# Attention and two MoE layers on one core: weight conversions moved out of three steps, four weight pieces moved behind the first MoE's last chunks

## The chip, the cores and the metric

One core of a Trainium2 chip runs the whole program. The metric is the device time of one execution in microseconds, as the median of several. The profiler took one execution of its own; its trace is read below, with times in us from the span's start.

## What is computed

The reference in short (4 batches, 8 heads, 576 positions, head width 64; then 2304 tokens of 512):

```python
scores = q @ k.T / sqrt(64) + decay(cumsum(log f))    # causal
x = softmax(scores) @ v                               # heads joined: 2304 x 512
h = maximum(maximum(x @ w1, x @ w2), x @ w3)          # 512 -> 768
x = h @ w_out                                         # 768 -> 512
h = x @ w_in                                          # 512 -> 2048
g = (a0 + a1*h + a2*h**2 + a3*h**3) / (1 + |b0|*|h| + |b1|*h**2 + 1e-6)
out = g @ w_out2                                      # 2048 -> 512
```

The weights arrive as 64-bit floats, so the kernel converts them itself, with integer operations on the bits. For accuracy most products are done in three matmuls, with a high and a low half of each operand.

## The kernel before

**Attention.** A *pair* is two heads of one batch and one or both groups of query positions (group 0: 320 columns, group 1: 256). Batch 0 comes first, as eight pairs of one group each: pairs 0 to 3 do group 0, pairs 4 to 7 group 1; batches 1 to 3 have four pairs of both groups each. Every head and group of a pair is a *slot*: slots 0 and 1 are pair 0, slots 6 and 7 are pair 3, the fourth. The main loop goes over steps. In step s the scores of slot s are computed (L388 to L391 on TensorE, row maximum on VectorE at L392, exponential on ScalarE at L399), slot s-1 is transposed (L432, evacuated at L434), and slot s-2 is multiplied with `v` when it is the second head of its pair (L448). So pairs 0 to 3 have their attention in steps 3, 5, 7 and 9. ScalarE then copies the high half of `x` (L455) and VectorE subtracts the low half (L456). For pairs 0 to 3 each bank is preceded by two matmuls that only keep TensorE exercised (L84).

**First MoE.** When all four pairs of a batch and group have their `x`, 22 units are put in a queue: 18 `h` units (six chunks `fc` of 128 columns times three weights, 12 matmuls each, L482 to L484) and four output units (L508 to L510). A running maximum goes through ScalarE (L488) and VectorE (L490); the third weight of a chunk leaves `hh`, the high half by ScalarE (L494) and the low half by GpSimd, or, in the tail, by VectorE (L496). `fill` is called six times in a step and places units at a steady pace: for the first group of batch 0 they go from step 9 to step 24.

**Conversions.** `conv` lists 30 of them: 18 of `w1` (the three input weights, 512 KB each) and 12 of `wo` (the output weight, 256 KB each). One conversion is an `Abs` on ScalarE (L181), four bit operations on VectorE (L186, L187, L188, L191), a copy for the high half on ScalarE (L197) and a subtraction for the low half on GpSimd (L200). `h` unit i needs item i; the output units need all of `wo`. `fill` also runs the conversions: `conv_due` adds 0.15 at each call in steps 0 to 6 and 0.5 from step 7 on. Two items are done before the loop. The raw data is loaded on SyncE's queue (L167) two items ahead; a raw `w1` piece takes one of six buffers of the tag `x2`, a raw `wo` piece one of eight of `x1`. From step 32 on, `conv2` does the second MoE's output weight by the same stages.

**Tail.** After the steps 44 units of the first MoE are left, group 0 and 1 of the last batch. Twelve are placed at once. Then a loop goes over 32 conversions of the second MoE's `w_in` (`conv3`, two pieces for each of the 16 chunks of 128 columns, four loads ahead) and places one unit behind every second of them; then come the units that remain. The second MoE follows: for each tile of tokens and each of 16 chunks `product` (L738 to L740), a gate on ScalarE and VectorE (L747 to L771) and `moe2_o` (L787 to L789) three chunks later.

**Who sets the order.** The program text gives each instruction a priority, and a planner, which simulates the engines with times of its own, lays down each engine's stream: of what is ready, the earlier in the text first, and the evacuations of the first MoE ahead of their place. On the chip each engine works off its stream in order. `keep_in_program_order` pins some instructions (the raw loads among them) to the order of the text. `tc.issue_after(ins)` puts an edge from `ins` to each instruction in its block that runs on the same engine: these come later in that engine's stream. It adds no semaphore.

Of the kernel before, what the change touches and what calls it, by code (L numbers as in the profile page):

```python
# [8 lines left out]
F32 = mybir.dt.float32  # L9
F32R = mybir.dt.float32r  # L10
I32 = mybir.dt.int32
AF = mybir.ActivationFunctionType
ALU = mybir.AluOpType
# [24 lines left out]
def kernel(  # L38
    ctx: ExitStack, tc: tile.TileContext, q, k, v, f, w1, w2, w3, w_out, m2_in, m2_out, m2_a, m2_b, out
):  # L40
    nc = tc.nc
    B, H, S, D = q.shape
# [5 lines left out]
    NF1 = FF1 // P  # L48
    NF2 = FF2 // P
    NPAIR = H // 2  # L50
    NB = len(Q0)

    def r32(ap):
        return ap.bitcast(F32)
# [67 lines left out]
    LOOK, WHOLE, PRE = 2, 6, 2  # L122
# [36 lines left out]
    E_LO, E_HI = 2.0**-15, float.fromhex("0x1.dffffep+16")  # L159

    raws = {}

    def load_raw(src, nm_):
        shape = list(src.shape)
# [4 lines left out]
    def stages(split, src, nm_, pool, tag, bufs, pin):  # L169
        shape = list(src.shape)  # L170
        at = {}

        def held(ins):
            return tc.keep_in_program_order(ins) if pin else ins

        def magnitude():
            raw = raws.pop(nm_)
            raw = raw.rearrange("p c (f t) -> p c f t", t=2)
            at["low"], at["top"] = raw[:, :, :, 0], raw[:, :, :, 1]
            at["t"] = pool.tile(shape, I32, name=f"cv_{nm_}", tag=tag, bufs=bufs)  # L180
            held(nc.scalar.activation(at["t"].bitcast(F32), at["top"].bitcast(F32), AF.Abs))  # L181

        def bits():
            t, low, top = at["t"], at["low"], at["top"]
            tf = t.bitcast(F32)
            held(nc.vector.tensor_scalar(tf, tf, E_LO, E_HI, op0=ALU.max, op1=ALU.min))  # L186
            nc.vector.tensor_scalar(t, t, 0x07FFFFFF, 3, op0=ALU.bitwise_and, op1=ALU.logical_shift_left)  # L187
            nc.vector.scalar_tensor_tensor(  # L188
                out=t, in0=low, scalar=29, in1=t, op0=ALU.logical_shift_right, op1=ALU.bitwise_or
            )  # L190
            nc.vector.scalar_tensor_tensor(  # L191
                out=t, in0=top, scalar=-0x40000000, in1=t, op0=ALU.bitwise_and, op1=ALU.bitwise_or
            )

        def high():
            at["hi"], at["lo"] = split()
            held(nc.scalar.activation(at["hi"], at["t"].bitcast(F32), AF.Copy))  # L197

        def low():
            held(nc.gpsimd.tensor_tensor(at["lo"], at["t"].bitcast(F32), r32(at["hi"]), op=ALU.subtract))  # L200

        return [magnitude, bits, high, low]
# [46 lines left out]
    def pipelined(work, look, begun=False):  # L249

        n = len(work)

        def go(i):
            for j in range(0 if i == 0 and not begun else i + look + (i == 0), min(i + look + 1, n)):
                work[j][0]()
            work[i][1]()

        return [lambda i=i: go(i) for i in range(n)]
# [99 lines left out]
    class Unit:  # L358
# [77 lines left out]
        def attend(self):  # L436

            p, h, g = self.pair, self.h, self.g
            if h == 0:
                return  # L440
            lo, hi = GQ[g]
            w = hi - lo
            ot = exercised(ps_o.tile([P, 512], F32, name=f"o_{self.nm}", tag="o"), p.n)
            order = list(GCH[g].items())
            with tc.high_priority():
                for j, (c, (col, q0)) in enumerate(order):
                    for i in (1, 0):
                        mm = nc.tensor.matmul(  # L448
                            ot[SIDES[i][0], q0 - lo : w], p.v[:, c, i], p.pt[g][:, i, col : col + hi - q0],
                            start=(j == 0), stop=(j == len(order) - 1),  # L450
                        )
                        if (j, i) != (0, 1):
                            pinned(mm)
            x = mpool.tile([P, 2, w], F32R, name=f"x_{self.nm}", tag=f"x{g}", bufs=(6, 8)[g])
            out_ = nc.scalar.activation(x[:, 0], ot[:, :w], AF.Copy)  # L455
            nc.vector.tensor_tensor(x[:, 1], ot[:, :w], r32(x[:, 0]), op=ALU.subtract)  # L456
            xt[p.b, p.hp, g] = x
            if p.b == 0:
                last["x"] = out_.ins


    hs = {}
# [12 lines left out]
    def moe1_h(b, g, fc, j):  # L475
        w = GQ[g][1] - GQ[g][0]
        nm_ = f"{b}_{g}_{fc}"
        xs = [xt[b, dc, g] for dc in range(NDC)]
        wh, wl = w1t[fc]
        hp_ = hbank(f"h{j}_{nm_}")  # L480
        for dc in reversed(range(NDC)):
            nc.tensor.matmul(hp_[:, :w], wh[:, j, dc], xs[dc][:, 1], start=(dc == NDC - 1), stop=False)  # L482
            nc.tensor.matmul(hp_[:, :w], wh[:, j, dc], xs[dc][:, 0], start=False, stop=False)  # L483
            nc.tensor.matmul(hp_[:, :w], wl[:, j, dc], xs[dc][:, 0], start=False, stop=(dc == 0))  # L484
        with tc.high_priority():
            nxt = mpool.tile([P, 320], F32, name=f"m{j}_{nm_}", tag="mx", bufs=3)
            if j == 0:
                nc.scalar.activation(nxt[:, :w], hp_[:, :w], AF.Copy)  # L488
            else:
                nc.vector.tensor_tensor(nxt[:, :w], cur[0][:, :w], hp_[:, :w], op=ALU.max)  # L490
            cur[0] = nxt
            if j == 2:
                hh = mpool.tile([P, 2, 320], F32R, name=f"hh_{nm_}", tag="hh", bufs=6)
                nc.scalar.activation(hh[:, 0, :w], nxt[:, :w], AF.Copy)  # L494
                eng = nc.gpsimd if tail["n"] is None else nc.vector
                eng.tensor_tensor(hh[:, 1, :w], nxt[:, :w], r32(hh[:, 0, :w]), op=ALU.subtract)  # L496
                hs[b, g, fc] = hh

    def moe1_o(b, g, dc):
# [17 lines left out]
    def moe1_units(b, g):  # L517
# [10 lines left out]
    conv = [  # L528
        (lambda fc=fc, j=j: load_raw(*raw_w1(fc, j)), lambda fc=fc, j=j: convert_w1(fc, j))
        for fc in range(NF1)  # L530
        for j in range(3)
    ]
# [2 lines left out]
        for fc in range(NF1)  # L535
        for z in range(2)
    ]
    ahead = [load_ for load_, _ in conv[: LOOK + 1]]
    conv = pipelined(conv, LOOK, True)
    wps = [(c, z) for c in range(NF2) for z in range(2)]  # L540
    conv2 = []
    for i, cz in enumerate(wps):
# [9 lines left out]
    units = []  # L552
    ready, ends = {}, {}
    NFILL = 6
    for n, p in enumerate(pairs):
        if p.hp == NPAIR - 1:
            at = first.get(n + 1, len(slots)) + 1
# [4 lines left out]
    state = {"m": 0, "of": 1, "n": 0}  # L562
# [22 lines left out]
    state["c"] = state["c2"] = 0.0  # L585

    def conv_due(step):
        state["c"] += 0.15 if step < 7 else 0.5
        return NCONV - int(state["c"])

    pairs[0].load()
# [14 lines left out]
    for step in range(len(slots) + 2):  # L606
        u = slots[step] if step < len(slots) else None
        t = slots[step - 1] if 0 <= step - 1 < len(slots) else None
        o = slots[step - 2] if 0 <= step - 2 < len(slots) else None
        prep, NPRE = [], 0  # L610
        if u is not None and u.pair.n + 1 < len(pairs):
            n = u.pair.n + 1
            at = first[n] - (2 if len(pairs[n - 1].groups) == 2 else PRE if pairs[n].whole else 1)
            if step == at:
                prep = pairs[n].prepare()
                NPRE = pairs[n].ng + 1
        if o:
            o.attend()
            if step in ready:
                queue.append((step, [x for bg in ready[step] for x in moe1_units(*bg)]))  # L620
        if step == 16:
            pinned(nc.sync.dma_start(ab[:, 0:4], m2_a.partition_broadcast(P)))
            pinned(nc.sync.dma_start(ab[:, 4:6], m2_b.partition_broadcast(P)))
        fill(step)
        if t:
            t.turn(0)
        fill(step)
        if t:
            for bank in range(1, len(GBANK[t.g])):
                t.turn(bank)  # L630
        fill(step)
        for f_ in prep[:NPRE]:
            f_()
        if u:
            blks = GBLK[u.g]
            u.begin()
            for i in blks[:-1]:
                u.scores(i)
            fill(step)
            u.scores(blks[-1])  # L640
        else:
            fill(step)
        fill(step)
        for f_ in prep[NPRE:]:
            f_()
        fill(step)
        if u:
            u.normalise()
        for p in lvat.get(step, []):
            p.load_v()  # L650
        if prep and n + 1 < len(pairs):
            pairs[n + 1].load()
    assert not conv and not conv2 and not units and len(queue) == 1
    units = queue.pop()[1]
# [3 lines left out]
    units = units[EARLY:]  # L658
# [4 lines left out]
    wih = w2pool.tile([P, NDC, FF2], F32R, name="wih")  # L663
    wil = w2pool.tile([P, NDC, FF2], F32R, name="wil")
    wpt = {}
    LOOK2 = 4

    def raw_wi(c, z):
        return rows(m2_in)[:, c : c + 2, z * P : (z + 1) * P], f"wi_{c}_{z}"
# [1 line left out]
    def convert_wi(c, z):  # L671
# [3 lines left out]
    conv3 = [  # L675
        (lambda c=c, z=z: load_raw(*raw_wi(c, z)), lambda c=c, z=z: convert_wi(c, z))
        for z in range(NF2)
        for c in (0, 2)
    ]
    for i, f_ in enumerate(pipelined(conv3, LOOK2)):  # L680
        f_()
        if units and i % 2 == 0:
            units.pop(0)()
# [181 lines left out]
```

## Time and profile before

| | us |
|---|---|
| median of 3 runs | 956.12 |
| lowest and highest | 954.08, 957.19 |
| the profiled execution | 953.65 |
| its span, first to last instruction | 951.6 |
| mean granted TensorE clock in it | 0.996 |

The stages in the trace: attention and first MoE together to some 472 us, the rest of the first MoE with the conversions of `w_in` to 552 us, the second MoE to the end. The profile's tables give busy time by engine and stretch, the timelines give instructions with the idle time before them and what released them. A matmul's row is longer than its share of TensorE, as matmuls are pipelined; the distance from start to start tells the rate.

### The profile page before, as it was taken

The page shows a single profiled execution, that of the slowest core. Times are in us where ns is not written, and L with a number is a line of the kernel's source. Part 1 is how long each engine was busy: PE and PEld are TensorE (multiplying, and loading weights), DVE is VectorE, ACT ScalarE, POOL GpSimd, SP SyncE. Part 2 cuts the span into 40 slices and gives each one's busy share as a digit, 9 for nine tenths or more (in the row PEclk, how much of TensorE's full clock was granted, in tenths as well). Part 3 has the DMA queues.
Part 4 walks back from the last instruction along what each step waited for, and adds up shares of the span by engine and source line. Part 5 has one row for each costly group of instructions (what it writes and reads, how often), then busy time and mean ns, then how long its engine had stood idle before and what let it go on. Part 6 is the DMA issues. An engine that isn't in the chain of part 4 may idle for free.

```text
span 951.6 us, 16833 instructions
## 1 busy us (share of the span) xinstructions
PE 930.5 (98%) x5780; PEld 825.3 (87%) x5780; DVE 723.0 (76%) x1692; ACT 648.8 (68%) x1542; POOL 241.3 (25%) x392
## 2 busy tenths in 40 slices
PE   6999999999999999999999999999999999999998
PEld 4758989988999989999999988888888888899997
DVE  8897854556776767534296969888888988899996
ACT  6898877767767676646354567667666766677765
POOL 4654424444555555414132300000000000000000
PEclk9989999999999999999999999999999999999999
DMA  7871431133556455220246386011002102100000
GB/s 192 227 229 52 111 106 45 44 87 102 149 151 194 124 159 165 65 79 2 68 145 192 118 296 235 1 45 45 0 1 70 42 1 67 44 1 1 34 1 34
DMA packets 125741, 88.52 MB, mean 93 GB/s; under 512 B 74572, under 2 KB 110424, under 8 KB 125656
## 3 DMA queue, kind: packets, MB, share of 16 engines
q1 hardware_dynamic: 125656, 87.45, 30.7%
q8 instruction: 46, 0.75, 0.3%
q14 instruction: 39, 0.32, 0.1%
HBM read 64.73 MB, written 22.69 MB: 92 GB/s over the span
## 4 chain that ended last, share of the span: by engine, by line
PE 84%; DVE 9%; ACT 2%; issue 2%; DMA 2%; SPq 1%; POOL 0%; ACTq 0%; DVEq 0%; POOLq 0%
PE hq L740 7%; PE oo L788 7%; PE hq L738 7%; PE hq L739 7%; PE oo L789 7%; PE oo L787 7%; PE h L482 6%; PE h L483 6%; PE h L484 6%; PE o L448 5%; PE tp L432 5%; PE x2p L508 2%; PE s L391 2%; PE s L390 2%; PE x2p L510 2%
## 5 line engine op out<-in xcount | busy, mean ns | idle before, releaser
L482 PE MATMUL h<-x,w1h 128*128 128x320 f32 (+1 forms) x576 | 175.7, 305 | 2.3 <-DVE x L456 2.0
L483 PE MATMUL h<-x,w1h 128*128 128x320 f32 (+1 forms) x576 | 172.2, 299 | 0.0
L484 PE MATMUL h<-x,w1l 128*128 128x320 f32 (+1 forms) x576 | 171.8, 299 | 0.0
L482 PEld LDWEIGHTS h<-x,w1h 128*128 128x128 f32 x576 | 109.2, 190 | 4.3 <-DVE x L456 2.3
L788 PE MATMUL oo<-wp,gh 128*128 128x512 f32 x288 | 112.7, 391 | 0.0
L399 ACT ACTIVATE e<-e,st 128x64 f32<-128x64 f32 (+4 forms) x160 | 89.0, 557 | 34.2 <-DVE st L392 33.0
L787 PE MATMUL oo<-wp,gh 128*128 128x512 f32 x288 | 112.1, 389 | 0.0
L747 ACT ACTIVATE s<-hq 128x512 f32<-128x512 f32 (+1 forms) x80 | 44.3, 554 | 97.6 <-PE hq L740 97.5
L483 PEld LDWEIGHTS h<-x,w1h 128*128 128x128 f32 x576 | 109.4, 190 | 0.4 <-issue 0.2
L484 PEld LDWEIGHTS h<-x,w1l 128*128 128x128 f32 x576 | 109.2, 190 | 0.0
L789 PE MATMUL oo<-wp,gl 128*128 128x512 f32 x288 | 109.2, 392 | 0.0
L412 POOL TENSOR_SCALAR e<-e,rs 128x64 f32<-128x64 f32 (+4 forms) x144 | 79.0, 563 | 103.3 <-DVE rs L406 87.8
L392 DVE CUSTOM_DVE_ANT_0 e<-s,mask 128x320 f32<-128x320 f32 (+3 forms) x160 | 67.0, 431 | 38.9 <-PE s L391 33.3
L750 DVE SCALAR_TENSOR_TENSOR s<-s,ab,u 128x512 f32<-128x512 f32 (+1 forms) x80 | 55.7, 697 | 32.3 <-ACT u L748 32.1
L434 ACT ACTIVATE pt<-tp 128x384 f32<-128x384 f32 (+3 forms) x160 | 69.4, 469 | 15.7 <-PE tp L432 14.0
L432 PE MATMUL tp<-ident,e 128*128 128x128 f32 (+1 forms) x480 | 75.8, 276 | 1.3 <-POOL e L412 0.9
L740 PE MATMUL hq<-x,wil 128*128 128x512 f32 (+1 forms) x192 | 69.9, 364 | 0.0
L738 PE MATMUL hq<-x,wih 128*128 128x512 f32 (+1 forms) x192 | 69.8, 364 | 0.0
L739 PE MATMUL hq<-x,wih 128*128 128x512 f32 (+1 forms) x192 | 69.7, 363 | 0.0
L789 PEld LDWEIGHTS oo<-wp,gl 128*128 128x128 f32 x288 | 54.1, 188 | 11.3
L787 PEld LDWEIGHTS oo<-wp,gh 128*128 128x128 f32 x288 | 54.1, 188 | 10.4
L788 PEld LDWEIGHTS oo<-wp,gh 128*128 128x128 f32 x288 | 54.1, 188 | 10.4
(133 smaller groups left out, 2433.3 us busy)
## 6 DMA issues: line engine op xcount, KB each, us to landing
raw_w<-in_moe_w_dram SPq DMA_DIRECT2D x18, 512.0 KB
raw_wp<-in_moe_w_out_dram SPq DMA_DIRECT2D x32, 256.0 KB
wpd<-wp SPq DMA_DIRECT2D x32, 256.0 KB
raw_wi<-in_moe_w_in_dram SPq DMA_DIRECT2D x32, 256.0 KB
wp<-wpd SPq DMA_DIRECT2D x10, 768.0 KB
x2d<-xo SPq DMA_DIRECT2D x16, 320.0 KB
out_dram<-ob SPq DMA_DIRECT2D x18, 256.0 KB
kn<-in_k_dram SPq DMA_DIRECT2D x32, 128.0 KB
```

The source lines that it names most:

```text
L399: nc.scalar.activation(e[:nr], e[:nr], AF.Exp, bias=m, scale=-1.0, accum_out=l)
L412: nc.gpsimd.tensor_scalar(e, e, self.rs[:, 1, j : j + 1], 0.0, op0=ALU.mult, op1=ALU.add)
L432: nc.tensor.transpose(tp[:kr, dst : dst + P], self.e[i][:, Q0[c] : Q1[c]], ident)
L482: nc.tensor.matmul(hp_[:, :w], wh[:, j, dc], xs[dc][:, 1], start=(dc == NDC - 1), stop=False)
L483: nc.tensor.matmul(hp_[:, :w], wh[:, j, dc], xs[dc][:, 0], start=False, stop=False)
L484: nc.tensor.matmul(hp_[:, :w], wl[:, j, dc], xs[dc][:, 0], start=False, stop=(dc == 0))
L738: nc.tensor.matmul(hp_[:, :w], wih[:, dc, fs], xh, start=(dc == 0), stop=False)
L739: nc.tensor.matmul(hp_[:, :w], wih[:, dc, fs], xl, start=False, stop=False)
L740: nc.tensor.matmul(hp_[:, :w], wil[:, dc, fs], xh, start=False, stop=(dc == NDC - 1))
L787: nc.tensor.matmul(o, g[0][:, ts_], wh_, start=(fc == 0), stop=False)
L788: nc.tensor.matmul(o, g[0][:, ts_], wl_, start=False, stop=False)
L789: nc.tensor.matmul(o, g[1][:, ts_], wh_, start=False, stop=(fc == NF2 - 1))
```

## The change

Three things are moved; the work is the same.

- `conv_due` adds nothing in steps 7 to 9, 1.0 at each call in steps 10 and 11, and 0.5 from step 12 on. In each of steps 7 to 9 one raw piece is loaded. From item 8 on the loads run five items ahead instead of two.
- `fourth["x"]` holds the ScalarE copy (L455) of the fourth pair's `x`. Every `Abs` that is placed after it gets an edge to it on ScalarE.
- In the tail `behind["hh"]` holds the VectorE instruction that makes the low half of `hh` for the last chunk of a group (L496): of group 0 from `conv3` item 16 on, of group 1 for the last three items, ahead of which all units that remain are placed. The first VectorE operation of those items (L186) gets an edge to it.

```diff
     raws = {}
+    behind = {"hh": None}
+    lows = {}
+    fourth = {"x": None}
...
-            held(nc.scalar.activation(at["t"].bitcast(F32), at["top"].bitcast(F32), AF.Abs))
+            with tc.issue_after(fourth["x"]) if fourth["x"] else nullcontext():
+                held(nc.scalar.activation(at["t"].bitcast(F32), at["top"].bitcast(F32), AF.Abs))
...
-            held(nc.vector.tensor_scalar(tf, tf, E_LO, E_HI, op0=ALU.max, op1=ALU.min))
+            with tc.issue_after(behind["hh"]) if behind["hh"] else nullcontext():
+                held(nc.vector.tensor_scalar(tf, tf, E_LO, E_HI, op0=ALU.max, op1=ALU.min))
...
                 last["x"] = out_.ins
+                fourth["x"] = fourth["x"] or (out_.ins if p.n == NPAIR - 1 else None)
...
-                eng.tensor_tensor(hh[:, 1, :w], nxt[:, :w], r32(hh[:, 0, :w]), op=ALU.subtract)
+                lows[b, g, fc] = eng.tensor_tensor(hh[:, 1, :w], nxt[:, :w], r32(hh[:, 0, :w]), op=ALU.subtract).ins
...
-    ahead = [load_ for load_, _ in conv[: LOOK + 1]]
-    conv = pipelined(conv, LOOK, True)
+    loads = [load_ for load_, _ in conv]
+    ahead = [loads.pop(0) for _ in range(LOOK + 1)]
+
+    def convert_next(i, run):
+        while loads and NC - len(loads) < i + (LOOK if i < HELD else FAR) + 1:
+            loads.pop(0)()
+        run()
+
+    NC, HELD, FAR = len(conv), 8, 5
+    conv = [lambda i=i, run=run: convert_next(i, run) for i, (_, run) in enumerate(conv)]
...
-        state["c"] += 0.15 if step < 7 else 0.5
+        state["c"] += 0.15 if step < 7 else 0.0 if step < 10 else 1.0 if step < 12 else 0.5
...
+        if 7 <= step < 10:
+            loads.pop(0)()
...
-    LOOK2 = 4
+    LOOK2, BETWEEN = 4, 16
...
     for i, f_ in enumerate(pipelined(conv3, LOOK2)):
+        if i == BETWEEN:
+            behind["hh"] = lows[B - 1, 0, NF1 - 1]
+        if i == len(conv3) - 3:
+            while units:
+                units.pop(0)()
+            behind["hh"] = lows[B - 1, 1, NF1 - 1]
         f_()
```

## Rows read from the trace of the kernel before

**Rows 1.** The page, busy us (share of the span) and instructions of each engine.

```profile
PE 930.5 (98%) x5780; PEld 825.3 (87%) x5780; DVE 723.0 (76%) x1692; ACT 648.8 (68%) x1542; POOL 241.3 (25%) x392
```

**Rows 2.** Table by stretch: busy us (instructions) of each engine, granted clock, DMA share, GB/s.

```profile
51.00:74.00 23.00, 19.03 (x84) 11.43 (x84) 23.00 (x51) 20.84 (x53) 13.50 (x13) 0.85 0.65 194
74.00:130.00 56.00, 55.45 (x397) 51.51 (x398) 40.65 (x121) 44.60 (x114) 23.77 (x33) 1.00 0.28 73
130.00:480.00 350.00, 347.10 (x2727) 322.15 (x2726) 207.04 (x683) 234.16 (x696) 155.27 (x281) 1.00 0.37 106
...
600.00:640.00 40.00, 40.00 (x178) 33.16 (x177) 35.01 (x54) 25.48 (x44) 0.00 (x0) 1.00 0.09 27
```

**Rows 3.** Timeline of PE, pairs 1 to 3: start, length, instruction, [idle before <- releaser].

```profile
41.74 1.41 PE L448 MATMUL o<-pt,v 128*64 128x320 f32 x12
...
50.91 1.41 PE L448 MATMUL o<-pt,v 128*64 128x320 f32 x12
...
66.40 2.62 PE L448 MATMUL o<-pt,v 128*64 128x320 f32 x12
...
70.66 1.54 PE L432 MATMUL tp<-ident,e 128*128 128x128 f32 x9
74.24 0.42 PE L482 MATMUL h<-x,w1h 128*128 128x320 f32 x1 [2.04 <-DVE x L456]
```

**Rows 4.** Timelines of DVE and, last row, of POOL in the same stretch.

```profile
45.04 0.49 DVE L456 TENSOR_TENSOR x<-o,x 128x320 fp32r<-128x320 f32 x1 [1.29 <-ACT x L455]
...
69.55 0.68 DVE L188 SCALAR_TENSOR_TENSOR cv_w<-raw_w,cv_w 128x512 int32<-128x512 int32 x1
...
70.49 1.76 DVE L188 SCALAR_TENSOR_TENSOR cv_w<-raw_w,cv_w 128x512 int32<-128x512 int32 x1
...
73.71 0.48 DVE L456 TENSOR_TENSOR x<-o,x 128x320 fp32r<-128x320 f32 x1
...
70.13 1.57 POOL L200 TENSOR_TENSOR w1l<-cv_w,w1h 128x512 fp32r<-128x512 f32 x1 [3.87 <-ACT w1h L197]
```

**Rows 5.** Conversions alone, DVE, ACT, POOL: `w1` twice, then `wo`, then `w_in`.

```profile
51.00:74.00 23.00, 19.54 (x28) 7.97 (x13) 8.91 (x7) 0.85 0.65 194
0.00:130.00 130.00, 50.12 (x72) 22.72 (x36) 24.97 (x18) 0.97 0.55 151
...
0.00:130.00 130.00, 18.98 (x48) 9.92 (x24) 8.98 (x12) 0.97 0.55 151
...
470.00:560.00 90.00, 51.76 (x128) 26.16 (x64) 25.76 (x32) 1.00 0.52 162
```

**Rows 6.** Timeline of PE at the end of the first MoE's two groups.

```profile
508.65 0.41 PE L508 MATMUL x2p<-hh,wo 128*128 128x320 f32 x1 [0.41 <-ACT hh L494]
...
542.57 0.28 PE L510 MATMUL x2p<-hh,wo 128*128 128x256 f32 x1
543.20 0.38 PE L508 MATMUL x2p<-hh,wo 128*128 128x256 f32 x1 [0.35 <-ACT hh L494]
...
544.38 0.39 PE L510 MATMUL x2p<-hh,wo 128*128 128x256 f32 x1 [0.68 <-DVE hh L496]
...
547.04 0.39 PE L508 MATMUL x2p<-hh,wo 128*128 128x256 f32 x1 [0.61 <-ACT hh L494]
```

**Rows 7.** Timeline of DVE around the same places, to the first gate.

```profile
504.98 0.83 DVE L186 TENSOR_SCALAR cv_wi<-cv_wi 128x256 f32<-128x256 f32 x1
...
508.62 0.67 DVE L496 TENSOR_TENSOR hh<-m,hh 128x320 fp32r<-128x320 f32 x1 [0.54 <-ACT hh L494]
...
538.61 0.83 DVE L186 TENSOR_SCALAR cv_wi<-cv_wi 128x256 f32<-128x256 f32 x1
...
547.02 0.72 DVE L496 TENSOR_TENSOR hh<-m,hh 128x256 fp32r<-128x256 f32 x1 [0.48 <-ACT hh L494]
...
556.72 0.75 DVE L750 SCALAR_TENSOR_TENSOR s<-s,ab,u 128x512 f32<-128x512 f32 x1 [3.04 <-ACT u L748]
```

**Rows 8.** Table by stretch, behind the first MoE's end.

```profile
550.00:555.00 5.00, 5.00 (x34) 4.59 (x33) 0.93 (x3) 0.86 (x3) 0.00 (x0) 1.00 0.83 242
```

## The prediction

> **What bounds the kernel now.** First the busy shares: TensorE (PE) is at 98% of the span, VectorE (DVE) at 76%, ScalarE (ACT) at 68% [rows 1]. A PE that is full everywhere leaves nothing to gain, so the next view is the table by stretch, to find where it is not full. From 130 to 480 us PE starts 2727 matmuls and idles 3 us in 350. In 51 to 74 us it starts 84 in 23 us, at a mean granted clock of 0.85 of the 2.4 GHz, while DVE is busy for all 23.00 us [rows 2]. That is place one: DVE-bound, with PE starving.
>
> Why it ends at 74 us: the first MoE's matmuls, which fill PE whenever attention waits, need `x` of all four pairs. The timeline of PE has the attention matmuls of pairs 1, 2 and 3 (steps 5, 7 and 9) at 41.74, 50.91 and 66.40 us: two steps took 9.2 us, and then 15.5 us [rows 3]. The low half of the fourth `x` starts on DVE at 73.71 [rows 4], and the first MoE matmul stands right behind it, at 74.24, after 2.04 us of waiting for that very `x` [rows 3].
>
> Place two is the end of the first MoE. Four times PE waits there for a chunk's `hh`: 0.41 us before 508.65, then 0.35, 0.68 and 0.61 us before 543.20, 544.38 and 547.04 [rows 6]. DVE, which makes the maxima and lows on that path, is at the time on pieces of the second MoE's `w_in` [rows 7]. The second MoE runs at PE's own rate, 178 matmuls in 40 us with no idle time [rows 2], so that an earlier start there is an earlier end.
>
> **Part one, the pause.** Before, 8 of the 30 conversions are placed by step 6, and 3 a step from step 7 on, to step 14. After: none in steps 7 to 9, six in each of steps 10 and 11 (10 of `w1`, 2 of `wo`), then 3 a step to step 15. No instruction goes away. The edge in ACT's order keeps each later `Abs` behind the copy of the fourth `x`, so that none slips forward into the pause; it is an order on one engine and waits for nobody else.
>
> What DVE is relieved of: 19.54 of its 23.00 us in 51 to 74 are `w1` conversions, 28 instructions, which is seven items of 2.8 us [rows 5]. Without them two steps should take the 9.2 us of the pair before, and the fourth attention starts at 60.1 instead of 66.40. Pair 1 needed 45.04 + 0.49 - 41.74 = 3.8 us from there to the end of its low half [rows 3, 4]; the MoE can start at 63.9, which is 10.3 us before 74.24. PE had meanwhile done work of later slots that it still has to do, 1.54 us of transposes from 70.66 [rows 3]. Cap of the gain: 8.8 us.
>
> What it costs later: by the means of the first 130 us (50.12 / 18 = 2.78 us of DVE and 22.72 / 18 = 1.26 of ACT for a `w1` item, 18.98 / 12 = 1.58 and 9.92 / 12 = 0.83 for a `wo` item) steps 10 and 11 carry 10 x 2.78 + 2 x 1.58 = 31.0 us of DVE and 14.3 us of ACT [rows 5]. PE's cover is eight MoE units whose weights are ready before the pause: 12 matmuls each at 350 / 2727 = 0.13 us [rows 2], 12.3 us, and more units as items come out. So I balance DVE. From 74 to 130 us it was busy for 40.65 of 56 us [rows 2]; with 19.5 us moved behind 63.9 it has 60.2 us to do in 66.1 us less the gain G. Packed without a hole, G is 5.9 us; work that slides past 130, where DVE is busy 207 of 350 us [rows 2], allows more, and each idle microsecond takes one off. I take 5.0 us, near the balance; ends 0 and 8.8.
>
> One row shows why an item costs 2.78 us and not less: L188 took 0.68 us at 69.55, and 1.76 us at 70.49, beside GpSimd's `w1l` from 70.13 to 71.70 [rows 4]. One such collision is 1.1 us; an item that meets none costs about 1.7 us, and ten of them would make G up to the cap. The Trainium skill, "SBUF — State Buffer", section "Who interferes with whom", speaks against crowding: a DVE instruction with two SBUF inputs and a reading GpSimd instruction exclude each other for the whole instruction. The trace agrees (1.76 against 0.68 us). By it each crowded item might meet one whole `w1l`, 1.39 us instead of 1.1; ten of those take 3 us off G, and the time would be near 951.5.
>
> Queues: what SP gets is the same loads, with five pieces ahead instead of two, three of them during the pause. A raw `w1` piece then takes the last of six buffers, so its load waits on SP for the conversion before it; behind it stand the next pairs' `v` loads and key rows, due about two steps later. I cost that at nothing, since all wait for those conversions anyway; without that cover it is one item, 2.8 us, once. GpSimd's lows (24.97 / 18 = 1.39 us each [rows 5]) move along on an engine busy 25% [rows 1].
>
> **Part two, the tail.** Each of the 32 `w_in` items is one `Abs`, four DVE operations, a copy and a GpSimd low. The order edge stands on the first DVE operation. Items 17 to 28 run behind 508.62, the low of group 0's last chunk, in the kernel before already; item 16 (from 504.98) ran before it, and items 29 to 31 (from 538.61 on) before the last low at 547.02 [rows 7]. These four move behind the lows: 4 x 51.76 / 32 = 6.5 us of DVE [rows 5] leave the two places. What PE gets back: the four idle times are 2.05 us, and a restart costs a little more (542.57 to 543.20 is 0.63 us where 0.12 is usual, so 0.51 lost with 0.35 idle [rows 6]), 0.16 x 4: 2.7 us. A chunk's own path over ACT and DVE remains, so I take 2.5 us; ends 1.0 (the largest wait and a half remain) and 2.7.
>
> Its price is hidden: between 550 and 555 us DVE is busy for 0.93 us [rows 8], and until 556.72 it waits 3.04 us for the first gate [rows 7]: 5.8 us of room for three pieces of 1.6 us. They are first used by the 15th chunk, some 300 matmuls after the second MoE begins, at 178 in 40 us 67 us later [rows 2]. Without that cover 4.9 us fall on DVE in the first gates.
>
> **Sum.** Against the profiled execution, 953.65 us (span 951.6 and 2 us around it): 953.65 - 5.0 - 2.5 = 946.15. The median of the runs, 956.12, stands 2.47 above that execution; predicted 948.6.
>
> **The rivals.** (a) *The pause pays in full*: 956.12 - 8.8 - 2.7 = 944.6 us. For it: collisions spread out, and late `wo` items can slide. Against it: the balance above. Chance 0.15. (b) *The hole only moves*: DVE holds PE up in steps 10 and 11 by as much as was saved; part one gives nothing, the tail 1.0 to 2.7, so 953.4 to 955.1; or the streams were in this order anyway, 956. For it: 31.0 us of items in two steps. Chance 0.2. (c) *Slower*: DVE's stream takes the twelve items strictly ahead of the reductions of slots 10 and 11. PE's cover is 12.3 us of units and 9.2 us for two steps; 31.0 - 21.5 = 9.5 us starved, 3.5 us by the lower clock (0.15 of 23 us, as in 51 to 74 [rows 2]) and five more collisions, 5.4 us: 18.4 lost against 8.8 and 2.5 won, 963.2 us. It decides from a hole of 11.3 us on. Against it: items 8 and on free further units as they come out. Chance 0.1. (d) My forecast, chance 0.55, own range 945.5 to 952.
>
> **Numbers.** A measurement of this kernel tells 0.3% (2.9 us, below 953.2) from no change. Faster: (a), (d) and a quarter of (b), 0.75. Within: the rest of (b), 0.15. Slower: (c), 0.10. The range 942.5 to 955.0 leaves out (c), the end of (b) at 956 and a little of (a), 2 in 10.
>
> **What would show it.** Right: no `cv_w` instruction on DVE between some 50 and 60 us; the fourth attention before 62 us and the first MoE matmul by 66; DVE at 100% for 25 to 30 us from there, with PE starting 30 matmuls or more in each 5 us. In the tail, no wait for `hh` over 0.3 us and the second MoE starting 2.5 us sooner after the last attention. Wrong: a second hole of PE between 70 and 100 us with waits for score reductions; a granted clock that falls for longer; first gates that wait for DVE.

## The result and the profile after

The changed kernel takes 962.31 us (median of 6 runs, 961.56 to 964.66) where the kernel before, run beside it, takes 955.8 us: a ratio of 1.0069 with a 95% interval of 1.0054 to 1.0083. It is slower by 6.5 us; predicted was 948.6 us, with 955.0 as the upper end of the range.

The profiled execution spans 960.5 us against 951.6 before. The page's first part (busy us, share, instructions) and the table by stretch of the changed kernel, to be laid beside [rows 1, 2]:

```profile
PE 933.7 (97%) x5780; PEld 826.8 (86%) x5780; DVE 727.2 (76%) x1692; ACT 648.6 (68%) x1542; POOL 240.8 (25%) x392
...
51.00:74.00 23.00, 21.61 (x127) 15.94 (x125) 14.14 (x41) 18.33 (x49) 3.77 (x7) 1.00 0.32 91
74.00:130.00 56.00, 49.15 (x328) 44.13 (x326) 54.34 (x120) 42.33 (x102) 31.14 (x35) 0.97 0.40 117
130.00:480.00 350.00, 345.23 (x2689) 317.82 (x2691) 206.95 (x686) 236.50 (x701) 156.24 (x282) 1.00 0.36 102
600.00:640.00 40.00, 40.00 (x178) 33.14 (x177) 34.77 (x54) 26.11 (x45) 0.00 (x0) 1.00 0.08 26
```

The hole at 51 to 74 us is nearly gone: PE starts 127 matmuls there instead of 84, at a granted clock of 1.00 instead of 0.85. But a new one stands in 74 to 130: PE 49.15 busy of 56 us where it had 55.45, and DVE 54.34 where it had 40.65. The second MoE keeps its rate.

PE's timeline at the same marks as [rows 3], and then five later marks (the attention of the fifth, the sixth, the eighth and the last pair, and the first matmul of the second MoE):

```profile
51.38 1.41 PE L453 MATMUL o<-pt,v 128*64 128x320 f32 x12
...
61.12 1.41 PE L453 MATMUL o<-pt,v 128*64 128x320 f32 x12
...
64.58 0.41 PE L488 MATMUL h<-x,w1h 128*128 128x320 f32 x1 [0.22 <-DVE x L461]
...
81.66 2.17 PE L453 MATMUL o<-pt,v 128*64 128x256 f32 x20
...
109.70 2.17 PE L453 MATMUL o<-pt,v 128*64 128x256 f32 x20
...
149.13 2.17 PE L453 MATMUL o<-pt,v 128*64 128x256 f32 x20
...
478.28 2.17 PE L453 MATMUL o<-pt,v 128*64 128x256 f32 x20
...
561.05 0.50 PE L760 MATMUL hq<-x2h,wih 128*128 128x512 f32 x1 [2.21 <-DVE xo L520]
```

The kernel before has these five at:

```profile
87.15 2.17 PE L448 MATMUL o<-pt,v 128*64 128x256 f32 x20
...
105.56 2.17 PE L448 MATMUL o<-pt,v 128*64 128x256 f32 x20
...
142.47 2.17 PE L448 MATMUL o<-pt,v 128*64 128x256 f32 x20 [0.20 <-ACT pt L434]
...
469.43 2.17 PE L448 MATMUL o<-pt,v 128*64 128x256 f32 x20
...
552.57 0.40 PE L738 MATMUL hq<-x2h,wih 128*128 128x512 f32 x1
```

So the first MoE starts 9.66 us sooner (64.58 for 74.24), and at the eighth pair (step 17) the changed kernel is 6.66 us behind: some 16 us are lost between these two marks. Of these, 9.63 us lie between the fifth and the sixth attention, which are 28.04 us apart instead of 18.41. Up to the last attention it is 8.85 us behind. Not all of this is the change's: in the profiles of the kernels below whose front part is that of the kernel before (tail_alone, tail_first_only, tail_behind_xo), the eighth pair lies at 143.55 to 145.13 instead of 142.47, and the last attention at 471.16 to 472.12 instead of 469.43. From the last attention to the second MoE both take the same: 83.14 before, 82.77 after; the kernels below with an unchanged tail take 82.5 to 83.9. In these profiles the loss is part one's, and part two gave nothing.

In the tail, the waits of PE from 500 to 575 us (us in total, times, longest): the waits for `hh` of [rows 6], 2.05 us, are down to 0.3, and one of 2.2 us for `xo` has come.

```profile
PE hq L760 <- DVE xo L520: 2.2, 1, 2.2
PE x2p L514 <- ACT hh L500: 0.3, 1, 0.3
```

### The profile page after: what moved, and what is told of

The parts are those of the page before. It is cut to its first block, busy times and chain, and to the rows that moved or that the text cites. A ratio compares the mean times of both kernels' runs of the same rounds, so it can differ in the third digit from the quotient of the medians.

```text
span 960.5 us, 16851 instructions
## 1 busy us (share of the span) xinstructions
PE 933.7 (97%) x5780; PEld 826.8 (86%) x5780; DVE 727.2 (76%) x1692; ACT 648.6 (68%) x1542; POOL 240.8 (25%) x392
## 4 chain that ended last, share of the span: by engine, by line
PE 78%; DVE 11%; ACT 5%; DMA 3%; issue 3%; POOL 0%; SPq 0%; ACTq 0%; DVEq 0%
PE hq L760 7%; PE hq L762 7%; PE oo L810 7%; PE hq L761 7%; PE oo L811 7%; PE oo L809 7%; PE h L488 5%; PE h L489 5%; PE h L490 5%; PE tp L437 4%; PE o L453 4%; PE s L396 2%; PE s L395 2%; PE x2p L514 1%; DVE cv_wi L193 1%
## 5 line engine op out<-in xcount | busy, mean ns | idle before, releaser
L417 POOL TENSOR_SCALAR e<-e,rs 128x64 f32<-128x64 f32 (+4 forms) x144 | 76.3, 544 | 109.0 <-DVE rs L411 91.2
```

The source lines that it names most:

```text
L417: nc.gpsimd.tensor_scalar(e, e, self.rs[:, 1, j : j + 1], 0.0, op0=ALU.mult, op1=ALU.add)
```

## The experiments

Ratios are to the kernel before, run beside each, with 95% intervals.

### Which part

> The pause, the edge on ScalarE and the early loads, without the edges in the tail. Theory (VectorE): the pause leaves VectorE idle for some 9 us where it is the engine that decides, ten items are moved and not seven, and the whole loss comes from here: 9 us slower than the kernel before, near 965, with the attention of the eighth pair 6 to 7 us later. Rival (tail): the tail's batch of three items is the loss, and this kernel is at 956 or faster.

The changed kernel without this piece of the tail's loop:

```diff
-        if i == BETWEEN:
-            behind["hh"] = lows[B - 1, 0, NF1 - 1]
-        if i == len(conv3) - 3:
-            while units:
-                units.pop(0)()
-            behind["hh"] = lows[B - 1, 1, NF1 - 1]
```

Measured: 961.16 us, 1.0056 [1.0040, 1.0073].

> The edges in the tail alone. Theory: the waits for hh go (2.5 us), and a wait of 2.2 us for the low half of xo takes their place, since three items stand ahead of it on VectorE: 0 to 0.7 us faster than before, 955 to 956; TensorE's wait ahead of the first hq is over 2 us. Rival (tail decides): several us slower than before.

The kernel before with that piece and `behind` and `lows`. Measured: 957.15 us, 1.0020 [1.0005, 1.0036], with the 2.2 us wait for `xo` as in the changed kernel. So part one costs 5.4 us by itself, and part two about 2 (0.5 to 3.4 by the interval), where both were to gain.

### The tail

> The tail's edge for item 16 on alone, nothing behind the second group. Theory: the wait of 0.4 us at the first group's end goes, the three waits at the second stay, no wait ahead of hq: 0.5 to 0.9 us faster than before. Rival (the first place does not matter): as before within 0.3 us.

Without the piece's second `if`. Measured: 955.25 us, 1.0006 [0.9995, 1.0016]: item 16's place gives nothing that can be told, and the waits for `hh` in the tail stay (3.1 us).

> The tail's edges alone, but the last three items stand behind the last low half of xo instead of the last low half of hh. Theory (the batch of three stands ahead of the xo lows, which free the xo buffers and the banks of the first hq): the wait of 2.2 us ahead of the first hq goes, the stretch from the last attention to the first hq is 2 to 3 us shorter than in tail_alone, 953 to 954.5. Rival (the banks come free late for another reason, such as the move to DRAM): the wait stays, 955 to 957.

```diff
-            nc.vector.tensor_tensor(xo[:, 1, :w], xp[:, :w], r32(xo[:, 0, :w]), op=ALU.subtract)
+            lows[b, g, "xo", dc] = nc.vector.tensor_tensor(xo[:, 1, :w], xp[:, :w], r32(xo[:, 0, :w]), op=ALU.subtract).ins
...
-            behind["hh"] = lows[B - 1, 1, NF1 - 1]
+            behind["hh"] = lows[B - 1, 1, "xo", NDC - 1]
```

Measured: 952.56 us, 0.9967 [0.9955, 0.9980]. DVE's timeline in the changed kernel, and then in this one, shows what the three pieces stood in front of:

```profile
552.92 0.42 DVE L502 TENSOR_TENSOR hh<-m,hh 128x256 fp32r<-128x256 f32 x1 [0.48 <-ACT hh L500]
553.26 0.69 DVE L191 TENSOR_SCALAR cv_wi<-cv_wi 128x256 f32<-128x256 f32 x3
553.87 0.69 DVE L192 TENSOR_SCALAR cv_wi<-cv_wi 128x256 int32<-128x256 int32 x3
554.47 1.09 DVE L193 SCALAR_TENSOR_TENSOR cv_wi<-raw_wi,cv_wi 128x256 int32<-128x256 int32 x3
555.48 1.09 DVE L196 SCALAR_TENSOR_TENSOR cv_wi<-raw_wi,cv_wi 128x256 int32<-128x256 int32 x3
556.49 0.72 DVE L722 TENSOR_SCALAR ab<-ab 128x4 f32<-128x4 f32 x1
557.12 0.74 DVE L520 TENSOR_TENSOR xo<-x2p,xo 128x256 fp32r<-128x256 f32 x2
560.57 0.42 DVE L520 TENSOR_TENSOR xo<-x2p,xo 128x256 fp32r<-128x256 f32 x1 [2.71 <-ACT xo L519]
```

```profile
545.51 0.42 DVE L499 TENSOR_TENSOR hh<-m,hh 128x256 fp32r<-128x256 f32 x1 [0.48 <-ACT hh L497]
546.99 0.76 DVE L517 TENSOR_TENSOR xo<-x2p,xo 128x256 fp32r<-128x256 f32 x2 [1.05 <-ACT xo L516]
...
551.89 0.69 DVE L189 TENSOR_SCALAR cv_wi<-cv_wi 128x256 f32<-128x256 f32 x3
```

In the changed kernel the first two `xo` lows follow the last `hh` low after 4.20 us (557.12 for 552.92), here after 1.48. They free what the next `xo` needs: ACT's copy for the third `xo` ends its wait at 560.15, for a transfer out of `xo`:

```profile
560.15 0.39 ACT L519 ACTIVATE xo<-x2p 128x256 fp32r<-128x256 f32 x1 [3.04 <-DMA x2d<-xo]
```

Behind that stand the lows at 560.57 and PE's first `hq`. With the pieces behind `xo`, the profile lists no wait of PE from 500 to 575 us, and the way from the last attention to the second MoE is 79.66 us (471.27 to 550.93) instead of 83.14.

### What does not carry part one's loss

> As pause_alone, without the edge on ScalarE behind the fourth x: only the counter rests, and the planner may take a conversion of step 10 earlier where ScalarE and VectorE have nothing else. Theory (VectorE's idle time decides): items slip into the idle time, VectorE is busier than 14.1 of 23 us in 51 to 74 us, and the kernel stands between before and pause_alone, 957 to 962. Rival (the counter's burst of twelve items decides, idle time or not): as pause_alone, near 965.

Part one without the edge on ACT (`fourth["x"]` stays `None`). Measured: 958.98 us, 1.0032 [1.0012, 1.0053]. Without the edge six items slip back into the pause (their lows end by 68 us), so that the fourth attention comes at 67.34 us: nothing is gained there, and 3.1 us are still lost, though only four items remain behind.

> As pause_alone, but 0.5 at each call from step 10 on, three items a step, instead of twelve in two steps. Rival (burst): without it the hole goes and the gain of the earlier fourth x stays, 946 to 952. Theory (VectorE's sum decides): the same idle time is lost and the same items come behind it, so 960 to 965, at most a few us better than pause_alone since reductions are no longer behind six items.

```diff
-        state["c"] += 0.15 if step < 7 else 0.0 if step < 10 else 1.0 if step < 12 else 0.5
+        state["c"] += 0.15 if step < 7 else 0.0 if step < 10 else 0.5
```

Measured: 963.93 us, 1.0085 [1.0067, 1.0102]. The burst in steps 10 and 11 is not the cause: without it the loss is no smaller, and by the medians it is 2.8 us larger (the intervals overlap).

> As pause_alone, but 1.0 at each call from step 10 to the end, so that the last conversion is placed in step 13 (before: step 14; pause_alone: step 15). New theory (supply): TensorE takes the first MoE's units well ahead of their pace, so what decides is when the conversions, wo above all, are done; with wo done earlier the loss of some 5 us between 130 and 140 us goes and 955 to 958 follows, though the hole at 90 to 100 us stays. Rival (VectorE's burst decides): still more items at once, 961 to 966.

The same line with 1.0 from step 10 to the end. Measured: 961.89 us, 1.0068 [1.0054, 1.0082]. A faster rate in the text brings nothing sooner: the last `wo` low ends at 135.4 us, as in pause_alone (135.8).

> As pause_alone, with loads two items ahead throughout and none of them in the pause, so that a raw w1 piece never needs the last of the six buffers and SyncE's queue is not held by it. Theory: loads do not decide, 960 to 963. Rival (SyncE's queue held the next pairs' loads and key rows behind raw pieces): 957 or faster.

Part one with the loads two items ahead, as before, and none in the pause. Measured: 960.21 us, 1.0046 [1.0029, 1.0062]. Most of the loss stays, so the loads and SP's queue are not it.

> The kernel before with one number changed: from step 7 on the counter adds 0.3 at each call instead of 0.5, no pause and no edge; items are spread to step 19, ahead of the units that need them (0.25 a call from step 9). Theory: VectorE is never idle in 51 to 74 us, has fewer items there, and uses its 15 idle us of 74 to 130 for the rest: the fourth x comes some 3 us earlier and 950 to 954 follows. Rival (each item that moves back costs as much later): 955 to 958.

The kernel before with 0.3 instead of 0.5 from step 7 on, and no pause. Measured: 965.24 us, 1.0104 [1.0084, 1.0123], the slowest of all: conversions that come late cost, with or without a pause.

> The kernel before without any pause of w1, with the twelve wo items placed in steps 10 to 15 instead of 10 to 14 (a rest of two thirds of a step, then 0.45 a call). Theory (supply): the output units of the first group come later, TensorE lacks work between 120 and 140 us, 958 to 961. Rival (the pause in steps 7 to 9, VectorE idle there, decides): no loss, 954 to 957.

The kernel before with its `w1` items in place and its `wo` items put off until step 11. Measured: 956.45 us, 1.0013 [1.0001, 1.0025]. With the last `wo` low at 129.7 us instead of 119.9, and `w1` as it was, 0.1 to 2.4 us are lost.

> The kernel before with 0.25 instead of 0.15 conversions at each call in steps 0 to 6: twelve items instead of eight by step 6, four fewer between there and step 14. Theory 'place': conversions are cheap where PE has no MoE units, so the hole at 51 to 74 us shrinks and nothing is paid later: 951 to 955. Rival 'loads': the data isn't there early, the items stand in the way of the first pairs: 956 to 961.

The kernel before with 0.25 instead of 0.15 in steps 0 to 6. Measured: 954.69 us, 0.9996 [0.9982, 1.0010]. The hole at 51 to 74 us shrinks (102 matmuls instead of 84), but the attention before it comes later: pair 2 at 58.4 us instead of 50.91. There was no free room in front either.

### DVE's work, taken away and moved

> As pause_alone, but the second of the four VectorE operations is left out of every conversion of w1 and wo (the values are no longer the weights; only the time is read): some 10 us less VectorE work behind the pause (10 x 0.57 and 12 x 0.38 us in the trace of the changed kernel). Theory (VectorE's sum behind the pause decides): most of the loss comes back, 952 to 956. Rival (loads, order or ScalarE decide): 959 to 961, as pause_alone.

```diff
-            nc.vector.tensor_scalar(t, t, 0x07FFFFFF, 3, op0=ALU.bitwise_and, op1=ALU.logical_shift_left)
+            if not nm_.startswith(("w0", "w1", "w2", "wo")):
+                nc.vector.tensor_scalar(t, t, 0x07FFFFFF, 3, op0=ALU.bitwise_and, op1=ALU.logical_shift_left)
```

Measured: 960.82 us, 1.0057 [1.0038, 1.0075].

> The kernel before with the same operation left out of the same 30 conversions. It tells what the saved VectorE work is worth without a pause: the hole of 51 to 74 us loses up to 7 x 0.7 us. Theory: 950 to 953, and the distance to pause_less_dve is smaller than the 6 us between pause_alone and before, 2 to 4 us. Rival (VectorE does not decide): 955, and the distance stays at 6 us.

The same line left out of the kernel before. Measured: 955.83 us, 0.9993 [0.9982, 1.0004]. One operation less changes neither kernel.

> Part one alone with two of the three integer operations of every w1 and wo conversion left out (the output isn't the reference's): between pause_less_dve (one left out, 960.8) and pause_light (three left out, 951.9). Theory 'DVE's work': the loss goes down with the work, somewhere between 953 and 958. Theory 'threshold elsewhere': it stays at 959 to 961 as with one left out, and only the last operation makes the step.

The line above and the first `scalar_tensor_tensor` put under the same `if`. Measured: 952.39 us, 0.9966 [0.9953, 0.9980].

> Part one alone, with the three integer operations of every w1 and wo conversion left out (the output isn't the reference's), so that an item has one DVE operation left instead of four, and ACT, GpSimd and the loads have all that they had. Theory 'conversions behind step 9': the items that the pause moves carry the loss through DVE's stream; some 50 us of DVE work are gone, so the pause gives its gain and little is paid later: 2 to 6 us below before_light. Theory 'order': the loss comes with the changed order of the attention's and the MoE's own work, or with ACT and GpSimd; the pause stays 3 to 6 us above before_light.

All three integer operations under it. Measured: 951.93 us, 0.9965 [0.9951, 0.9979].

> The kernel before, with the same three operations left out (the output isn't the reference's): the yardstick for pause_light. If DVE's work alone makes the hole at 51 to 74 us, the fourth attention comes by 62 us and the time is 949 to 952. If the items wait for loads, ACT or GpSimd there, the hole stays and the time is 954 to 956.

The same three left out of the kernel before. Measured: 953.33 us, 0.9983 [0.9962, 1.0004]. So with almost no DVE work on the weights the pause is 1.4 us below its yardstick (the intervals overlap, so that this small gain isn't sure), where with all of that work it is 5.4 us above. The loss hangs on DVE's work for the conversions, and not on ACT's, GpSimd's or the loads by themselves, of which all remained, nor on the order in the text. It isn't in proportion: one operation less does nothing, two take the loss away. (The kernel before with two left out was not run; with one and with three it stands at 0.9993 and 0.9983.)

> Part one with the pause in steps 8 and 9 only, and the faster rate in step 10 only: three items fewer are moved. If the loss goes with the number of items moved behind step 9 (ten in part one, +5.4 us), three fewer are worth some 2 to 4 us: 956.5 to 959.5. If any pause costs the same, 960 to 962.

```diff
-        state["c"] += 0.15 if step < 7 else 0.0 if step < 10 else 1.0 if step < 12 else 0.5
+        state["c"] += 0.15 if step < 7 else 0.5 if step == 7 else 0.0 if step < 10 else 1.0 if step < 11 else 0.5
```

Measured: 956.11 us, 1.0001 [0.9989, 1.0014]. Three `w1` items fewer are moved, seven instead of ten, and all of the loss is gone. No gain is left either, though the fourth attention comes at 62.03 us. By the count alone pause_no_edge, with four behind, should then lose nothing; it loses 3.1 us, so the count isn't the whole of it.

Nor is the sum of DVE's work. Behind 62 us DVE has 43.85 us of conversions in pause_short (17.89 of `w1` and 25.96 of `wo`) and 42.38 in pause_less_dve (19.72 and 22.66), against 51.72 in pause_alone. With nearly the same work, pause_short loses nothing and pause_less_dve 5.5 us.

The table by stretch, 74 to 104 and 104 to 150 us (PE, PEld, DVE, ACT, POOL busy, instructions; granted clock, DMA share, GB/s), of before, pause_alone, pause_short and pause_mid in turn:

```profile
74.00:104.00 30.00, 29.45 (x205) 27.51 (x206) 23.30 (x67) 24.15 (x62) 13.97 (x18) 1.00 0.29 80
104.00:150.00 46.00, 45.35 (x341) 41.88 (x340) 27.91 (x95) 35.23 (x97) 15.71 (x30) 1.00 0.35 92
```

```profile
74.00:104.00 30.00, 25.29 (x162) 22.60 (x160) 29.64 (x56) 22.91 (x52) 18.43 (x18) 0.94 0.46 133
104.00:150.00 46.00, 41.53 (x293) 36.02 (x293) 38.49 (x111) 36.32 (x100) 19.62 (x30) 1.00 0.39 107
```

```profile
74.00:104.00 30.00, 24.45 (x167) 21.47 (x166) 29.15 (x60) 21.73 (x53) 19.02 (x20) 1.00 0.30 89
104.00:150.00 46.00, 44.19 (x319) 38.86 (x319) 34.51 (x102) 35.50 (x100) 16.21 (x28) 1.00 0.35 88
```

```profile
74.00:104.00 30.00, 26.69 (x179) 24.64 (x178) 23.11 (x46) 24.34 (x60) 18.38 (x20) 0.94 0.35 100
104.00:150.00 46.00, 44.50 (x326) 40.64 (x325) 27.03 (x88) 36.76 (x103) 17.81 (x32) 0.96 0.37 98
```

Two tolls are to be seen. From 74 to 104 us DVE is full in both pauses (29.64 and 29.15 of 30 us), and PE is busy for 4 to 5 us less: the gain at 51 to 74 is paid back there. From 104 to 150 us pause_alone loses another 3.8 us against before, pause_short only 1.2. With DVE at 23.11 us (pause_mid) the first toll is smaller and the second is 0.85. The counts of matmuls say it more plainly, as PE's busy time also holds the slower rows of a lower clock. Against before, pause_alone starts 42 more from 51 to 74 us, 43 fewer to 104 and 48 fewer to 150, so 49 fewer in all; pause_short 46 more, 38 fewer and 22 fewer, so 14 fewer; pause_mid is 4 ahead. Kernels with the front part of before (tail_alone, tail_first_only, tail_behind_xo) are 8 to 14 behind it in the same count, so pause_short as a whole can't be told from them.

### Both parts in their best form

> Both parts, each in its best form so far: the pause in steps 8 and 9 with the faster rate in step 10 only, and the last three w_in pieces behind the last chunk's xo lows. If the two parts add up, 956.1 - 3.2 = 952.9; if the pause in any form spoils the tail, 955 or more.

The changed kernel with the edits of pause_short and tail_behind_xo. Measured: 952.47 us, 0.9975 [0.9962, 0.9989]. The two parts add up, and the pause in its best form adds nothing to tail_behind_xo's 0.9967. Both kernels beat the one before; what they gain is the tail's.

## Why the prediction was wrong

**Up to the fourth attention it was right.** That attention came at 61.12 us (60.1 forecast), the first MoE matmul at 64.58 (63.9), the clock stayed at 1.00, and no conversion stood on DVE in the pause.

**The step that failed is the balance of part one ("So I balance DVE"): its first number, and the reading of DVE's room as time gained.** The first number: "with 19.5 us moved behind 63.9" counted the seven items that fill 51 to 74 us. But the first eight items are all that the change leaves in front, and the kernel before had finished ten by 51 us. Two rows of its DVE, the last operations of the ninth and the tenth:

```profile
42.65 0.69 DVE L191 SCALAR_TENSOR_TENSOR cv_w<-raw_w,cv_w 128x512 int32<-128x512 int32 x1
...
49.91 0.68 DVE L191 SCALAR_TENSOR_TENSOR cv_w<-raw_w,cv_w 128x512 int32<-128x512 int32 x1
```

So ten items move. In the changed kernel DVE's `w1` conversions, up to the first `h` and from there on:

```profile
0.00:64.00 64.00, 22.49 (x32) 1.00 0.71 189
64.00:150.00 86.00, 28.53 (x40) 0.98 0.39 113
```

The 28.53 us replace the 2.05 us of `w1` among the 40.65, and the `wo` items became dearer as well, 23.23 us instead of 18.98. By these the balance is 40.65 - 2.05 + 28.53 + 4.25 = 71.4 us of work in 66.1 us less G: G is below zero, by 5.3 us, before any hole in the packing. My number for the items stood in [rows 5]; what it stood for (instructions in a stretch) was not what the change moves (items after the eighth), though the "10 x 2.78" just ahead of the balance had the right count. The pause itself left DVE idle for 8.9 of 23 us, 8.05 of them before 64 us, where the balance doesn't begin.

That these 5.3 us come so near to part one's 5.4 is luck, for with the right numbers the balance fails elsewhere. pause_short moves just seven items, as I had counted; by the same sum it would gain 66.1 - (40.65 - 2.05 + 17.89 + 6.98) = 2.6 us (with the forecast's own terms 5.0), and it gains nothing (1.0001). pause_less_dve would gain 66.1 - (40.65 - 2.05 + 19.72 + 3.68) = 4.1 us, and it loses 5.5. The count explains at most why the changed kernel is worse than pause_short; that room on DVE up to 130 us is no gain of PE's is the larger error.

**The second failure is what DVE's fullness does.** I let G be what is left over on DVE, and only the rivals (b) and (c) let DVE hold PE up, which is what happened. (c) priced it by a whole-step queue, with "items 8 and on free further units as they come out" against it. The rows show that the units are no sure cover: their own evacuations queue as well. DVE of the changed kernel:

```profile
93.54 0.47 DVE L496 TENSOR_TENSOR m<-m,h 128x320 f32<-128x320 f32 x1
93.93 1.81 DVE L196 SCALAR_TENSOR_TENSOR cv_w<-raw_w,cv_w 128x512 int32<-128x512 int32 x1
95.67 0.68 DVE L193 SCALAR_TENSOR_TENSOR cv_w<-raw_w,cv_w 128x512 int32<-128x512 int32 x1
96.27 0.28 DVE L192 TENSOR_SCALAR cv_wo<-cv_wo 128x256 int32<-128x256 int32 x1
96.47 0.47 DVE L318 TENSOR_TENSOR k2s<-tk,k1s 64x320 fp32r<-64x320 f32 x1
96.87 1.16 DVE L191 TENSOR_SCALAR cv_wo<-cv_wo 128x256 f32<-128x256 f32 x1
97.95 0.47 DVE L496 TENSOR_TENSOR m<-m,h 128x320 f32<-128x320 f32 x1
```

and its PE:

```profile
98.48 0.55 PE L488 MATMUL h<-x,w1h 128*128 128x320 f32 x1 [2.40 <-DVE m L496]
98.83 0.47 PE L489 MATMUL h<-x,w1h 128*128 128x320 f32 x1
99.09 0.47 PE L490 MATMUL h<-x,w1l 128*128 128x320 f32 x1
```

Between the maximum at 93.54 and the one at 97.95 DVE does four conversion operations, 3.93 us by their rows (which overlap a little), and one split. PE waits 2.40 us with its next `h`, the very work that was to cover the burst, and then goes on at a lower clock: from 99 to 101 us the granted clock is 0.50 (1.2 GHz), and a row starts 0.26 to 0.27 us after the one before it, where at 1.00, from 94.3 to 95.8 us, it was 0.15. After step 9 every step has more that DVE must hand to PE (`m`, `k2s`, `q1s`, `st`, later `xo`); in the pause's place there was only attention. I had priced the cover (12.3 us of units) as if units were PE's alone. From 74 to 104 us such waits for `m` come to 3.6 us in the changed kernel.

The 1.81 us at 93.93 are one of the collisions that I counted. GpSimd's rows beside it:

```profile
93.92 1.28 POOL L205 TENSOR_TENSOR w1l<-cv_w,w1h 128x512 fp32r<-128x512 f32 x1
```

The operation takes 0.69 us alone, so this one cost 1.12 us, which agrees with the 1.1 us of the text.

The forecast of (c), 963.2 us, is near the measured 962.31, with the chance at 0.1 too low; the nearness is partly luck. Its terms are not confirmed one by one: its hole of 9.5 us right behind the burst was 4.2 us by 104 and nearly as much again by 150, and spreading the burst made it no better, which (c) did not say. Its "strictly ahead of the reductions of slots 10 and 11" fits the sixth pair, which is these two slots and comes 28.04 us behind the fifth instead of 18.41. The sign that I named, a second hole between 70 and 100 us, is there; its waits are mostly for `m`, and 0.7 us are for score reductions.

**Part two's failed term is its price.** The gain was there: of 2.05 us of waits 0.3 were left, and with the pieces put elsewhere the stretch got 3.5 us shorter (83.14 to 79.66). That is more than my upper end of 2.7, and where the rest comes from is not shown. "Its price is hidden: between 550 and 555 us DVE is busy for 0.93 us" was the mistake. That idle time [rows 8] belongs to a chain: the lows of `xo`, with their transfers, lie in it, and a piece that is ordered behind the `hh` low runs ahead of them. Three pieces took 3.3 us there (553.26 to 556.57), the first `xo` lows came 2.7 us later, and PE's first `hq` waited 2.21 us. I said the pieces had until the 15th chunk, which is true; I didn't ask what stood behind them on DVE.

**What stays open.** That DVE's work on the weights carries part one's loss is shown: with nearly half of it left out (pause_mid, 28.21 of 51.72 us behind 62 us) the loss is gone. That its amount decides is not shown (pause_short and pause_less_dve have nearly the same), nor by which chain the second toll (104 to 150 us) reaches PE. The operation that makes the step between pause_less_dve and pause_mid is also one that collides with GpSimd's lows [rows 4], and no run takes fewer collisions apart from less work. The kernels line up, though roughly, by when the first MoE's weights are complete, here by the ends of GpSimd's last lows:

| kernel | last `w1` low, us | last `wo` low, us | ratio |
|---|---|---|---|
| before_light | 71.1 | 114.2 | 0.9983 |
| early | 75.8 | 113.1 | 0.9996 |
| before_late_wo | 80.4 | 129.7 | 1.0013 |
| pause_light | 99.2 | 115.6 | 0.9965 |
| pause_mid | 102.2 | 123.7 | 0.9966 |
| pause_short | 101.7 | 127.6 | 1.0001 |
| pause_less_dve | 109.6 | 133.3 | 1.0057 |
| pause_near_loads | 106.6 | 135.6 | 1.0046 |
| pause_no_edge | 111.0 | 134.7 | 1.0032 |
| pause_alone | 111.1 | 135.8 | 1.0056 |
| pause_fast | 111.5 | 135.4 | 1.0068 |
| pause_spread | 118.3 | 141.8 | 1.0085 |
| steady | 109.4 | 162.0 | 1.0104 |

The kernel before has 80.3 and 119.9. With the last `wo` by 128 us nothing is lost, at 129.7 at most 2.4 us, and from 133 us on 3 to 10 us. That would fit output units which wait on PE for `wo` while nothing else is left to fill it, and it would explain the step between pause_less_dve and pause_mid. But the last `w1` moves with it in all pauses, and the one kernel that moves `wo` alone reaches only 129.7 us. No run separates the two, so this is an order that fits, not a cause that is shown.

The traces speak against it for pause_alone. PE's `h` matmuls (us busy, count; granted clock, DMA share, GB/s) in the kernel before, and then in pause_alone:

```profile
0.00:125.00 125.00, 36.59 (x216) 0.97 0.57 156
125.00:150.00 25.00, 3.20 (x24) 1.00 0.40 108
```

```profile
0.00:125.00 125.00, 37.91 (x216) 0.97 0.57 156
125.00:150.00 25.00, 0.00 (x0) 1.00 0.34 93
```

The 216 are all of the first group, so both have done them by 125 us; of the output units' matmuls both have done as many by then (14 and 15) and by 150 us (74 each). So at 125 us pause_alone is level in MoE work, and behind with attention: its sixth pair stands at 109.51 us instead of 105.56. From there on no `h` unit is left to cover attention's waits until the eighth pair releases the next group, whose first matmul comes at 152.74 us instead of 146.28. Of PE's waits from 104 to 150 us the profile puts only 0.4 us down to `wo`. In pause_spread, by contrast, 1.9 us are put down to `wo` and 3.1 to `w1`. So late weights can be the chain there; in pause_alone it looks more like attention that the moved work holds back, and no run tests that by itself.

## What to carry to other kernels

Before an edit moves work out of a hole, count what it moves by the program's own index (which items lie behind the new point), not by what the hole holds; then balance the receiving stretch with that sum. Room that is left over is not yet a gain, as pause_short shows. A filler is cover only if its own helpers on the full engine have room: a matmul unit whose evacuation queues behind the moved work stalls in the place where it was to help. And idle time on an engine at a hand-over is not room: look at what it waits for there, and put moved work behind the last link of that chain, as tail_behind_xo did.

## What the runs showed of the hardware

An undisturbed `w1` item costs 2.22 us of DVE, by the medians of its four operations in the changed kernel (0.420, 0.426, 0.688 and 0.690 us), not the 1.7 us of my text; so collisions with GpSimd, if all that exceeds it is theirs, are worth 0.56 us an item by the mean of 2.78 before, and packing the items behind one another left that as it was (28.53 / 10 = 2.85). It was the `wo` items that got dearer beside them, from 18.98 / 12 = 1.58 to 23.23 / 12 = 1.94 us. Three `w_in` pieces done in one row on DVE, operation by operation, took 3.3 us, 1.1 each, where the mean between the first MoE's work is 51.76 / 32 = 1.62 [rows 5].
